# Low part of each head's q on GpSimd, and silu's product ahead of the block's maxima on VectorE, in a kernel of windowed attention and a gated feed-forward

## The chip, the core and the metric

The kernel runs on one core of a Trainium2 chip. The metric is the device time of one execution in microseconds (us), as the median of several runs. Of the core's engines, TensorE (PE) multiplies matrices, VectorE (DVE), ScalarE (ACT) and GpSimd (POOL) do the elementwise work, and SyncE (SP) issues the transfers. Each engine takes its instructions in the order in which the program wrote them for it, and waits at one whose inputs aren't there or whose output space isn't free.

## The reference

Attention over 8 batches, 8 heads, 576 positions and 64 dimensions a head, with a window of 32 positions in the first four heads and of every fourth position in 128 in the others; then a normalised, gated feed-forward over the 4608 tokens of width 512, with 1536 hidden columns:

```python
scores = where(mask, (q @ k.T) / sqrt(64), -1e9)
attn = softmax(scores) @ v                     # -> x: 4608 x 512
rms = sqrt(mean(x * x, -1) + 1e-6)
xn = x / rms * rms_g
g = xn @ w_gate
val = xn @ w_val
out = (g * sigmoid(g) * val) @ w_out
```

All inputs and outputs are float32.

## The kernel before, in words

The 4608 tokens are cut into 16 units of 288 (half a sequence). The feed-forward of unit u runs on TensorE while the attention of unit u + 1 is worked off in between, so the feed-forward of each of the units 2 to 14 has nearly the same pattern in time (even and odd units differ in the number of keys).

**The steps.** The feed-forward of a unit has 12 hidden blocks j of 128 columns, and each block three steps: part 0 is `gate` (the product for g), part 1 is `val`, part 2 is `proj` (the output product of the block before, into four accumulators `acc`). A step of a unit from 1 on is 12 matmuls of 128 x 288: four pieces of 128 rows, times three products. The three come from the way in which float32 is kept: each operand is split into a high part, rounded to the faster type fp32r, and a low part, the rest; high x high, low x high and high x low are added up.

**Attention in between.** After a step's 12 matmuls come those of the attention that are due: scores `s` (L508, L511), transposes `t` of the normalised probabilities (L486), outputs `o` (L495, L499, L500), at the sum of squares `rps` and its spreading `bps` (L601). A unit has 14 attention blocks, begun about every second step. The work of a block: maxima on VectorE (`scores_max`: L379 adds the mask, L384 takes the maximum of each of two heads), exponentials on ScalarE (L395), row sums and reciprocals on VectorE (L404, L405), division on GpSimd (L411), transposition on TensorE, high and low parts of the transposed on ScalarE (L466) and VectorE (L468), and the output: copied by ScalarE (L431), and its second half added by VectorE (L441, in `add`). From unit 3 on (`NEX = 3`) q and k are split too: `split` takes the high parts on ScalarE (L348 for k, L357 for q) and the low parts elsewhere (`k_lo` L353, `q_lo` L362). The q and k of a head come in one transfer with their two copies on 128 partitions; q's low part is wanted on the upper 64 alone, so `q_lo` works on 64 x 288. When `q_lo` is written the transfer of the head two further on is issued too.

**What sets the order.** Nothing is reordered by a scheduler. `later(dt, rank, fn)` puts `fn` on a list for the step dt ahead; at the start of each step `flush` runs that step's list in the order of rank (lower first, equal ranks in the order of entry), before the step's matmuls are written. The ranks that matter here: reciprocals -1, `add` of outputs -0.3, tanh and `prod` 0, transposes' copy 0.2, low part of the transposed 0.4, `normal` and `part` (the normalised input) 0.6, `scores_max` 0.7, `silu` 0.8, `q_lo` 0.9, `k_lo` 5. `tanh`, `silu` and the maxima of a block that was scored in part 0 stand in one flush, that of part 1. For odd j a block is scored in part 0; for even j it is scored elsewhere.

**Who holds what.** `gate` and `val` share two banks of PSUM in turn, and the transposes use the bank that is next free: the bank of gate j is free when `silu` (L697) has read it, then may hold a transposed block until L468 has read that, and is then that of val j + 1. The output `o` has one bank, free when `add` (L441) has read it. `th` holds tanh, then silu, then the product with val (`prod`, L710), and has one buffer: the next tanh waits until the high part (`hhi`, L721 on ScalarE) and the low part (`hlo`, L722 on GpSimd) are taken from it. The input's low parts `xlo` are made in `part` (L633), those of two pieces on VectorE and of two on GpSimd.

The functions that the change touches, and what calls them:

Of the kernel before, what the change touches and what calls it, by code (L numbers as in the profile page):

```python
# [29 lines left out]
NEX = 3  # L30
# [31 lines left out]
def geometry(u, c):  # L62


    half = u % 2
    if c < NC // 2:
        if half:
            return [(QB * i, QB * i, 0, P) for i in range(U // QB)], QB, U + W
        return [(QB * i, max(QB * i - W, 0), 0 if i else W, P if i else QB)
                for i in range(U // QB)], QB, U  # L70
    nq = U // DIL
    keys = nq + (W if half else 0)
    return [(nq * r, keys * r, 0 if half else W, keys) for r in range(DIL)], nq, keys * DIL
# [3 lines left out]
def attn_moe(ctx: ExitStack, tc: tile.TileContext, qk_in, v_in, w_gate, w_val, w_out, rms_g, outT):  # L77
# [4 lines left out]
    V, A, G, PE = nc.vector, nc.scalar, nc.gpsimd, nc.tensor  # L82
# [36 lines left out]
    def later(dt, rank, fn):  # L119
        put_off.setdefault(now[0] + dt, []).append((rank, fn))  # L120
# [164 lines left out]
    def load(u, h):  # L285

        _, _, nkt = geometry(u, h // 2)
        if u < NEX and h % 4 > 1:
            raw = sb.tile([P, 2 * KW], F32, tag="ks", name=f"qk_{u}_{h}", bufs=3)
        else:  # L290
            raw = sb.tile([P, U + KW], F32, tag="qk", name=f"qk_{u}_{h}", bufs=2)
        nc.sync.dma_start(out=raw[:, :U + nkt], in_=qk_in[u, h][:, :U + nkt])
        heads[u, h] = raw
# [35 lines left out]
    def after(u, h, n):  # L329

        k = u * H + h + n
        return divmod(k, H) if k < NU * H else None

    def split(u, h, when, ek, eq):


        raw = heads[u, h]
        _, _, nkt = geometry(u, h // 2)
        qr, kr = raw[:, :U], raw[:, U:U + nkt]
        got = []  # L340

        def tile(cols, tag):
            pool, bufs = (late[0], 1) if late and h % 4 == 3 else (sb, 3)
            return pool.tile([P, cols], F32R, tag=tag, name=f"{tag}_{u}_{h}", bufs=bufs)

        def k_hi():
            ks = tile(2 * KW, "ks").rearrange("p (t k) -> p t k", t=2)
            A.copy(out=ks[:, 0, :nkt], in_=kr)  # L348
            got.append(ks)

        def k_lo():
            ks = got[0]
            ek.tensor_tensor(out=ks[:, 1, :nkt], in0=kr, in1=ks[:, 0, :nkt], op=ALU.subtract)  # L353

        def q_hi():
            qs = tile(U, "qs")
            A.copy(out=qs, in_=qr)  # L357
            got.append(qs)

        def q_lo():  # L360
            ks, qs = got
            eq.tensor_tensor(out=qs[D:], in0=qr[D:], in1=qs[D:], op=ALU.subtract)  # L362
            heads[u, h] = (qs, ks)
            if after(u, h, 2):
                load(*after(u, h, 2))

        for dt, rank, fn in zip(when, (3, 5, 3.1, 0.9 if when[3] > when[2] else 3.2), (k_hi, k_lo, q_hi, q_lo)):
            later(dt, rank, fn)
# [66 lines left out]
    def add(u, c, i, o):  # L435
        _, nq, _ = geometry(u, c)
        x = xraw[u, c]
        to = x[:, QB * i:QB * i + nq] if c < NC // 2 else x.rearrange("p (j r) -> p r j", r=DIL)[:, i, :]
        for a in range(2):
            rows = slice(a * D, (a + 1) * D)  # L440
            V.tensor_tensor(out=to[rows], in0=o[rows, a * nq:(a + 1) * nq], in1=to[rows], op=ALU.add)  # L441
# [31 lines left out]
    def products(q, t, o, t_ps, s_tag="s", o_tag="o", wait=False):  # L473


        if q:
            s_ps = ps.tile([P, 512], F32, tag=s_tag, name=f"s_{q[0]}_{q[1]}_{q[2]}")
        if o:
            o_ps = ps.tile([P, 512], F32, tag=o_tag, name=f"o_{o[0]}_{o[1]}_{o[2]}")
            pt = st.pop(o)  # L480
        if t:
            p, _ = st.pop(t)
        def transposed(a):
            blocks, nq, _ = geometry(*t[:2])
            n = blocks[t[2]][3]
            PE.transpose(t_ps[:n, a * QB:a * QB + nq], p[:nq, a, :n], ident[:nq, :nq])  # L486

        def output(a):
            blocks, nq, _ = geometry(*o[:2])
            n = blocks[o[2]][3]  # L490
            if a:
                return
            out = o_ps[:, :2 * nq].rearrange("d (a q) -> d a q", a=2)
            if o[0] < NEX:
                PE.matmul(out, vs.pop(o)[:n].rearrange("k a d -> k (a d)"), pt[:n, 0, :, :nq], start=True, stop=True)  # L495
                return
            vh, vl = (part[:n].rearrange("k a d -> k (a d)") for part in vparts[everything.index(o) % 2])
            both = o_ps[:, :4 * nq].rearrange("d (t a q) -> d t a q", t=2, a=2)
            PE.matmul(both, vh, pt[:n, :, :, :nq], start=True, stop=False)  # L499
            PE.matmul(out, vl, pt[:n, 0, :, :nq], start=False, stop=True)  # L500

        def scored(a):
            blocks, nq, _ = geometry(*q[:2])
            qc, kc, _, n = blocks[q[2]]
            sv = s_ps[:QB].rearrange("q (a t k) -> q a t k", a=2, t=2)
            if q[0] < NEX:
                qk = heads[q[0], 2 * q[1] + a]
                PE.matmul(sv[:nq, a, 0, :n], qk[:, qc:qc + nq], qk[:, U + kc:U + kc + n], start=True, stop=True)  # L508
                return
            qs, ks = heads[q[0], 2 * q[1] + a]  # L510
            PE.matmul(sv[:nq, a, :, :n], qs[:, qc:qc + nq], ks[:, :, kc:kc + n], start=True, stop=True)  # L511

        order = ((t, transposed), (o, output), (q, scored))
        if t and t[0] >= NEX:
            order = ((o, output), (t, transposed), (q, scored))
        parts = [(b, fn, a) for b, fn in order for a in range(2)]
        for b, fn, a in parts:
            if b:
                fn(a)
        if t:  # L520
            later(1, 0.2, lambda: untranspose(t, t_ps, wait))
        if o:
            later(1, 0.5, lambda: take(*o, o_ps))
            if o[0] >= NEX:
                later(2, -0.3, lambda: add(*o, o_ps))
            if o[0] < NEX:
                later(1, 9, lambda: load_v(further(o, 3)))
            far = further(o, 2)
            if far and far[0] >= NEX:
                split_v(far, 8 if o[0] < NEX else 1)  # L530
        if q:
            later(1, 0.7, lambda: scores_max(*q, s_ps))
            later(2, 2, lambda: scores_exp(*q))
            later(3 if q[0] < NNAT else 4, -1, lambda: scores_norm(*q))
            u, c, i = q
            nxt = after(u, 2 * c, 2)
            nb = len(geometry(u, c)[0])
            if u < NEX:
                if u == NNAT - 1 and c == NC - 1 and i == nb - 1:
                    for h in range(4):  # L540
                        later(1, 9, lambda h=h: load(NNAT, h))
                if u >= NNAT and i == nb - 1 and c < NC - 1:
                    for a in range(2):
                        later(1, 9, lambda a=a: load(*after(u, 2 * c + a, 4)))
                if u == NEX - 1 and c == NC - 1 and i == nb - 1:
                    for a in range(2):
                        later(3 + a, 9, lambda a=a: split(NEX, a, (1, 2, 2, 3), G, V))
            elif nxt and i == 0:
                split(*nxt, (1, 2, 2, 3), G, V)
                split(nxt[0], nxt[1] + 1, (2, 3, 3, 4), G, V)  # L550

    xs = {}
    NB = U // QB
# [125 lines left out]
    def gate(u, j):  # L679
        g_ps = group("g", u, j)  # L680
        if u == 0:
            used.append(("g", j))
        g = g_ps[:, :U]

        def tanh():
            nonlocal g
            t = (sb.tile([P, U], F32, tag="hhi", name=f"h_{j}", bufs=2) if u == 0 else
                 sb.tile([P, U], F32, tag="th", name=f"th_{u}_{j}", bufs=1))
            if u + j == 0:
                g = sb.tile([P, U], F32, tag="hhi", name="g_first", bufs=2)  # L690
                V.tensor_tensor(out=g, in0=g_ps[:, :U], in1=root[0], op=ALU.mult)
            A.activation(out=t, in_=g, func=AF.Tanh, scale=0.5)  # L692
            gv[u, j] = t

        def silu():
            t = gv[u, j]
            V.scalar_tensor_tensor(out=t, in0=t, scalar=1.0, in1=g, op0=ALU.add, op1=ALU.mult)  # L697

        later(1, 0 if u + j else 0.65, tanh)
        later(1, 0.8, silu)  # L700
        return g_ps[:, U:U + 2 * QB]

    def val(u, j):
# [220 lines left out]
```

## Time and profile before

| what | value |
|---|---|
| median of 3 runs | 1148.53 us (1148.25 to 1151.82) |
| profiled execution | 1148.96 us |
| its span, from the first instruction to the last | 1146.8 us, 2.2 us less than its time |
| TensorE busy | 1122.0 us, 98% of the span |
| VectorE, ScalarE, GpSimd busy | 736.7, 702.7 and 597.5 us (64, 61 and 52%) |
| granted TensorE clock | 1.000 throughout |
| DMA engines | 23.5% |

A matmul's time in the profile runs from its start to an end that is modelled, and the next one starts before that end. A stretch in which TensorE was kept waiting thus shows as a start that comes late after the start before it, and the idle time given in brackets is only the part of it that lies behind the modelled end. Times in the rows of a timeline are in us from the start of the span.

### The profile page before, as it was taken

How to read it: one execution, taken by the hardware profiler on the slowest of the kernel's cores; microseconds unless marked ns; L12 is line 12 of the kernel's file. 1: busy time of each engine (PE TensorE's matmuls, PEld its weight loads, DVE VectorE, ACT ScalarE, POOL GpSimd, SP SyncE). 2: the span in 40 equal slices, each digit the busy share in tenths (PEclk: the TensorE clock that was granted, in tenths of full speed). 3: DMA queues.
4: the chain of work that ended last, by engine and by line, in shares of the span. 5: the costliest groups of instructions: out<-in, count | busy, mean ns of one | idle time of the engine just before them, and what ended most of it. 6: DMA issues, size and time to landing. Idle time of an engine off the chain costs nothing.

```text
span 1146.8 us, 25563 instructions
## 1 busy us (share of the span) xinstructions
PE 1122.0 (98%) x8362; PEld 1078.3 (94%) x8362; DVE 736.7 (64%) x2838; ACT 702.7 (61%) x2579; POOL 597.5 (52%) x1050
## 2 busy tenths in 40 slices
PE   7999999999999999999999999999999999999998
PEld 5787999999999999999999999999999999999998
DVE  7889778656575665757656575665757656575412
ACT  6795667657576665756656565665656656565311
POOL 7423577555465554646556465564546555464211
PEclk9999999999999999999999999999999999999999
DMA  9664312212131121212212131131212212120000
GB/s 258 180 250 164 96 45 76 64 33 79 41 99 40 50 84 40 79 41 62 69 39 82 40 92 42 48 90 38 76 40 62 78 34 77 42 79 15 3 19 22
DMA packets 61542, 82.17 MB, mean 72 GB/s; under 512 B 7298, under 2 KB 41090, under 8 KB 61410
## 3 DMA queue, kind: packets, MB, share of 16 engines
q1 hardware_dynamic: 61410, 80.54, 23.5%
q8 instruction: 67, 1.10, 0.4%
q14 instruction: 65, 0.53, 0.2%
HBM read 71.08 MB, written 9.44 MB: 70 GB/s over the span
## 4 chain that ended last, share of the span: by engine, by line
PE 74%; DVE 12%; ACT 7%; POOL 3%; issue 2%; DMA 1%; SPq 0%; DVEq 0%; POOLq 0%; ACTq 0%
PE acc L655 13%; PE g L655 13%; PE v L655 12%; PE acc L652 7%; PE g L652 7%; PE v L652 6%; PE s L511 2%; PE o L499 2%; DVE qs L362 2%; PE acc L649 2%; PE v L649 2%; PE t L486 2%; PE g L649 2%; DVE t L379 2%; DVE t L384 2%
## 5 line engine op out<-in xcount | busy, mean ns | idle before, releaser
L722 POOL TENSOR_TENSOR hlo<-th,hhi 128x288 fp32r<-128x288 f32 x179 | 145.7, 814 | 213.0 <-ACT hhi L721 206.6
L655 PE MATMUL acc<-hhi,lo 128*128 128x288 f32 x720 | 212.6, 295 | 0.0
L411 POOL TENSOR_SCALAR t<-t,sum 72x72 f32<-72x72 f32 (+3 forms) x414 | 151.8, 378 | 67.1 <-DVE sum L405 52.5
L721 ACT CAST hhi<-th 128x288 fp32r<-128x288 f32 x180 | 78.0, 433 | 171.2 <-DVE th L710 171.2
L323 POOL TENSOR_TENSOR vlo<-vt,vhi 128x128 fp32r<-128x128 f32 x182 | 87.2, 479 | 178.8 <-ACT vhi L319 177.3
L655 PE MATMUL g<-xhi,lo 128*128 128x288 f32 x612 | 180.3, 295 | 0.0
L655 PE MATMUL v<-xhi,lo 128*128 128x288 f32 x612 | 180.2, 294 | 0.0
L395 ACT ACTIVATE t<-t,sum 96x128 f32<-96x128 f32 (+3 forms) x448 | 165.2, 372 | 11.4 <-DVE sum L384 10.9
L692 ACT ACTIVATE th<-g 128x288 f32<-128x288 f32 x180 | 73.6, 409 | 127.2 <-PE g L486 72.3
L697 DVE SCALAR_TENSOR_TENSOR th<-th,g 128x288 f32<-128x288 f32 x180 | 81.1, 450 | 92.1 <-ACT th L692 57.9
L655 PEld LDWEIGHTS acc<-hhi,lo 128*128 128x128 f32 x720 | 135.4, 188 | 0.0
L441 DVE TENSOR_TENSOR xraw<-o,xraw 64x72 f32<-64x72 f32 (+1 forms) x364 | 97.1, 267 | 39.0 <-ACT xraw L431 35.9
L655 PEld LDWEIGHTS g<-xhi,lo 128*128 128x128 f32 x612 | 115.2, 188 | 0.0
L655 PEld LDWEIGHTS v<-xhi,lo 128*128 128x128 f32 x612 | 115.1, 188 | 0.0
L379 DVE TENSOR_TENSOR t<-s,mask 96x256 f32<-96x256 f32 (+3 forms) x182 | 66.7, 366 | 73.9 <-PE s L511 63.7
L652 PE MATMUL acc<-hhi,hi_o 128*128 128x288 f32 x360 | 109.1, 303 | 0.0
L652 PE MATMUL g<-xhi,hi_g 128*128 128x288 f32 x357 | 106.9, 300 | 0.8 <-DVE th L710 0.8
L710 DVE TENSOR_TENSOR th<-th,v 128x288 f32<-128x288 f32 x180 | 80.9, 450 | 40.5 <-PE v L655 35.5
L655 PE MATMUL acc<-hlo,hi_o 128*128 128x288 f32 x360 | 106.4, 296 | 0.0
L431 ACT COPY xraw<-o 64x72 f32<-64x72 f32 (+1 forms) x364 | 95.4, 262 | 11.8 <-PE o L500 9.7
L353 POOL TENSOR_TENSOR ks<-qk,ks 128x288 fp32r<-128x288 f32 (+2 forms) x104 | 96.9, 936 | 1.9 <-ACT ks L348 1.6
L655 PE MATMUL g<-xlo,hi_g 128*128 128x288 f32 x322 | 95.1, 295 | 0.0
(188 smaller groups left out, 3525.6 us busy)
## 6 DMA issues: line engine op xcount, KB each, us to landing
qk<-in_qk_dram SPq DMA_DIRECT2D x60, 288.0 KB, 2.9
vt<-in_v_dram SPq DMA_DIRECT2D x196, 64.0 KB, 1.8
qk<-in_qk_dram SPq DMA_DIRECT2D x30, 352.0 KB, 3.0
out_dram<-ot SPq DMA_DIRECT2D x64, 144.0 KB, 1.9
qk<-in_qk_dram SPq DMA_DIRECT2D x30, 304.0 KB, 2.9
raw<-in_w_gate_dram SPq DMA_DIRECT2D x12, 512.0 KB, 6.4
raw<-in_w_val_dram SPq DMA_DIRECT2D x12, 512.0 KB, 6.4
raw<-in_w_out_dram SPq DMA_DIRECT2D x12, 512.0 KB, 4.6
```

Of the source, the lines that this page charges most:

```text
L323: G.tensor_tensor(out=vl, in0=vs.pop(b), in1=vh, op=ALU.subtract)
L353: ek.tensor_tensor(out=ks[:, 1, :nkt], in0=kr, in1=ks[:, 0, :nkt], op=ALU.subtract)
L379: V.tensor_tensor(out=t[:nq, :, :n], in0=sv[:nq, :, 1, :n], in1=mask[:nq, None, mc:mc + n].to_broadcast([nq, 2, n]), op=ALU.add)
L395: A.activation(out=t[:nq, a, :n], in_=t[:nq, a, :n], func=AF.Exp, scale=-1.0, bias=sm[:nq, a, 0:1], accum_out=sm[:nq, a, 1:2] if u or i % ...
L411: (V if u == 0 and (c, i) > (NC - 1, 0) else G).tensor_scalar(out=t[:nq, a, :n], in0=t[:nq, a, :n], scalar1=sm[:nq, a, 3:4], scalar2=1.0, ...
L431: A.copy(out=to[a * D:(a + 1) * D], in_=o[a * D:(a + 1) * D, (2 + a) * nq:(3 + a) * nq])
L441: V.tensor_tensor(out=to[rows], in0=o[rows, a * nq:(a + 1) * nq], in1=to[rows], op=ALU.add)
L652: PE.matmul(out, wh[:, cc, :], xh, start=start, stop=False)
L655: PE.matmul(out, w[:, cc, :], v, start=False, stop=stop and k == 1)
L697: V.scalar_tensor_tensor(out=t, in0=t, scalar=1.0, in1=g, op0=ALU.add, op1=ALU.mult)
L710: V.tensor_tensor(out=t, in0=t, in1=v_ps[:, :U], op=ALU.mult)
L722: (V if (u, j) == (NU - 1, NJ - 1) else G).tensor_tensor(out=lo, in0=t, in1=hi, op=ALU.subtract)
```

## The change

There are two edits. In `split`, the engine that takes q's low part is given by the caller, and in all four calls it becomes GpSimd (`G`) where it was VectorE (`V`). The calls concern units 3 to 15, so 104 instructions. And `silu` gets rank 0.6 where it had 0.8, for all units of the feed-forward but the first, so that it is written ahead of `scores_max` (0.7) where both stand in one flush.

```diff
                     for a in range(2):
-                        later(3 + a, 9, lambda a=a: split(NEX, a, (1, 2, 2, 3), G, V))
+                        later(3 + a, 9, lambda a=a: split(NEX, a, (1, 2, 2, 3), G, G))
             elif nxt and i == 0:
-                split(*nxt, (1, 2, 2, 3), G, V)
-                split(nxt[0], nxt[1] + 1, (2, 3, 3, 4), G, V)
+                split(*nxt, (1, 2, 2, 3), G, G)
+                split(nxt[0], nxt[1] + 1, (2, 3, 3, 4), G, G)
...
         later(1, 0 if u + j else 0.65, tanh)
-        later(1, 0.8, silu)
+        later(1, 0.6 if u else 0.8, silu)
```

What this does to the order in which the instructions stand is seen at three places. The first is VectorE around the last hidden block (j = 11) of a unit, before: the names are those of the program with their buffers' numbers (`th_11` is tanh of block 11, `t_1_1` the scores of piece 1, block 1, `qs_4` the parts of q of head 4, `pt` the transposed, `spare` and `xlo` parts of the next unit's input). Each L384 row stands a second time, for the second head.

```order
L615 SCALAR_TENSOR_TENSOR xraw_3_8603<-xraw_3_8603,gs,bps_8879 128x288
L379 TENSOR_TENSOR t_1_1_8983<-s_1_1_8970,mask 96x256
L384 ISA t_1_1_8983,sum_86<-s_1_1_8970,t_1_1_8983 96x128
L384 ISA sum_86 96x1
L697 SCALAR_TENSOR_TENSOR th_11_8975<-th_11_8975,g_11_8957 128x288
L362 TENSOR_TENSOR qs_4_8954<-qk_4_8798,qs_4_8954 64x288
L404 TENSOR_REDUCE sum_90<-sum_90 96x2
L405 RECIPROCAL sum_90<-sum_90 96x2
L710 TENSOR_TENSOR th_11_8975<-th_11_8975,v_11_8994 128x288
L468 TENSOR_TENSOR pt_0_1_8977<-g_11_8957,pt_0_1_8977 128x192
L633 TENSOR_TENSOR xlo_3_9017<-xraw_3_8603,spare 128x288
L362 TENSOR_TENSOR qs_5_8991<-qk_5_8837,qs_5_8991 64x288
```

And VectorE at the same place with the change:

```order
L615 SCALAR_TENSOR_TENSOR xraw_3_8603<-xraw_3_8603,gs,bps_8879 128x288
L697 SCALAR_TENSOR_TENSOR th_11_8975<-th_11_8975,g_11_8957 128x288
L379 TENSOR_TENSOR t_1_1_8984<-s_1_1_8970,mask 96x256
L384 ISA t_1_1_8984,sum_86<-s_1_1_8970,t_1_1_8984 96x128
L384 ISA sum_86 96x1
L404 TENSOR_REDUCE sum_90<-sum_90 96x2
L405 RECIPROCAL sum_90<-sum_90 96x2
L710 TENSOR_TENSOR th_11_8975<-th_11_8975,v_11_8994 128x288
L468 TENSOR_TENSOR pt_0_1_8977<-g_11_8957,pt_0_1_8977 128x192
L633 TENSOR_TENSOR xlo_3_9017<-xraw_3_8603,spare 128x288
L468 TENSOR_TENSOR pt_0_2_9046<-t_11_9037,pt_0_2_9046 128x192
```

Both L362 are gone, and silu (L697) stands ahead of the maxima, behind the input's normalisation (L615). The same holds for j = 1, 3, 5 and 9; for j = 10 silu passes one L615, and elsewhere silu keeps its place.

The second place is VectorE in block j = 4, where the next chunk's scores begin, before:

```order
L468 TENSOR_TENSOR pt_2_2_9453<-t_3_9444,pt_2_2_9453 104x2x72
L379 TENSOR_TENSOR t_3_1_9460<-s_3_1_9445,mask 72x2x104
L384 ISA t_3_1_9460,sum_88<-s_3_1_9445,t_3_1_9460 72x104
L384 ISA sum_88 72x1
L362 TENSOR_TENSOR qs_0_9429<-qk_0_9196,qs_0_9429 64x288
L404 TENSOR_REDUCE sum_87<-sum_87 72x2
L405 RECIPROCAL sum_87<-sum_87 72x2
L441 TENSOR_TENSOR xraw_2_9457<-o_2_0_9446,xraw_2_9457 64x72 x2
L697 SCALAR_TENSOR_TENSOR th_4_9493<-th_4_9493,g_4_9474 128x288
L362 TENSOR_TENSOR qs_1_9467<-qk_1_9231,qs_1_9467 64x288
L710 TENSOR_TENSOR th_4_9493<-th_4_9493,v_4_9501 128x288
```

With the change the two L362 rows are gone here and nothing else moves: the maxima and silu stand in different flushes. The third place is GpSimd around j = 11, in the changed kernel:

```order
L353 TENSOR_TENSOR ks_4_8927<-qk_4_8798,ks_4_8927 128x416
L633 TENSOR_TENSOR xlo_2_8980<-xraw_2_8358,xhi_2_8979 128x288
L362 TENSOR_TENSOR qs_4_8954<-qk_4_8798,qs_4_8954 64x288
L353 TENSOR_TENSOR ks_5_8952<-qk_5_8837,ks_5_8952 128x416
L411 TENSOR_SCALAR t_1_0_8923<-t_1_0_8923,sum_90 96x128 x2
L722 TENSOR_TENSOR hlo_11_9014<-th_11_8975,hhi_11_9013 128x288
L362 TENSOR_TENSOR qs_5_8991<-qk_5_8837,qs_5_8991 64x288
L323 TENSOR_TENSOR vlo_2278<-vt_0_2_8652,vhi_2277 128x128
```

The two L362 rows are new there: one stands between the low parts of two heads' k, the other behind the low part of the hidden block (L722). The orders of TensorE, ScalarE and SyncE are as before.

## The prediction

> **What bounds the kernel now.** I read the page's first part, then the waits of TensorE, then the timelines of four engines over one pattern of two units, which repeats.
>
> ```profile
> span 1146.8 us, 25563 instructions
> PE 1122.0 (98%) x8362; PEld 1078.3 (94%) x8362; DVE 736.7 (64%) x2838; ACT 702.7 (61%) x2579; POOL 597.5 (52%) x1050
> ...
> PE o L499 <- DVE xraw L441: 4.5, 12, 0.4
> PE bps L601 <- ACT rd L585: 3.1, 13, 0.3
> PE v L652 <- DVE pt L468: 2.4, 7, 0.3
> ```
>
> TensorE is busy 98% of the span, and the change leaves its instructions alone, so all that can be won is time in which it is kept waiting. The waits (total in us, times, longest) come 7, 12 and 13 times, 13 units split q, even and odd in turn: bps waits in all of them, v in the 7 even ones, o in 6 of either kind. They show only what lies behind the modelled end of the matmul before, so I take the lateness from the starts. One pattern, near 600 us, in an even unit ("A"):
>
> ```profile
> 603.53 0.25 PE L500 MATMUL o<-pt,vlo 128*128 128x192 f32 x1
> 603.82 0.36 PE L486 MATMUL t<-ident,t 96*128 96x96 f32 x2
> ...
> 605.71 0.29 PE L655 MATMUL g<-spare,lo 128*128 128x288 f32 x1
> 606.35 0.40 PE L652 MATMUL v<-xhi,hi_g 128*128 128x288 f32 x1 [0.34 <-DVE pt L468]
> ...
> 612.20 0.25 PE L500 MATMUL o<-pt,vlo 128*128 128x192 f32 x1
> 612.29 0.33 PE L486 MATMUL g<-ident,t 96*128 96x96 f32 x2
> ...
> 616.03 0.25 PE L500 MATMUL o<-pt,vlo 128*128 128x192 f32 x1
> 616.34 0.36 PE L486 MATMUL t<-ident,t 96*128 96x96 f32 x2
> ...
> 629.41 0.29 PE L655 MATMUL g<-xlo,hi_g 128*128 128x288 f32 x1
> 629.55 0.29 PE L655 MATMUL g<-spare,lo 128*128 128x288 f32 x1
> 629.92 0.40 PE L652 MATMUL v<-xhi,hi_v 128*128 128x288 f32 x1
> ...
> 631.48 0.29 PE L655 MATMUL v<-spare,lo 128*128 128x288 f32 x1
> 632.14 0.37 PE L499 MATMUL o<-pt,vhi 104*128 104x288 f32 x1 [0.36 <-DVE xraw L441]
> ```
>
> A start follows the last after 0.13-0.14 (629.41 to 629.55), a transpose after 0.09 (612.20 to 612.29). So TensorE comes late by 0.29 - 0.09 = 0.20 at 603.82, 0.64 - 0.13 = 0.51 at 606.35, 0.31 - 0.09 = 0.22 at 616.34, 0.37 - 0.13 = 0.24 at 629.92 and 0.66 - 0.13 = 0.53 at 632.14. In the odd unit ("B") two of the same places:
>
> ```profile
> 675.11 0.29 PE L655 MATMUL g<-xhi,lo 128*128 128x288 f32 x1
> 675.47 0.40 PE L652 MATMUL v<-xhi,hi_g 128*128 128x288 f32 x1
> ...
> 700.03 0.29 PE L655 MATMUL v<-xhi,lo 128*128 128x288 f32 x1
> 700.71 0.37 PE L499 MATMUL o<-pt,vhi 72*128 72x288 f32 x1 [0.39 <-DVE xraw L441]
> ```
>
> 0.36 - 0.13 = 0.23 and 0.68 - 0.13 = 0.55. All these wait for VectorE, whose queue there is:
>
> ```profile
> 600.46 0.42 DVE L379 TENSOR_TENSOR t<-s,mask 96x256 f32<-96x256 f32 x1 [0.58 <-PE s L511]
> ...
> 601.81 0.86 DVE L362 TENSOR_TENSOR qs<-qk,qs 64x288 fp32r<-64x288 f32 x1
> 603.33 0.35 DVE L468 TENSOR_TENSOR pt<-g,pt 128x192 fp32r<-128x192 f32 x1
> 604.24 1.18 DVE L633 TENSOR_TENSOR xlo<-xraw,spare 128x288 fp32r<-128x288 f32 x1 [0.56 <-ACT spare L632]
> 605.45 0.46 DVE L362 TENSOR_TENSOR qs<-qk,qs 64x288 fp32r<-64x288 f32 x1
> 605.94 0.36 DVE L468 TENSOR_TENSOR pt<-t,pt 128x192 fp32r<-128x192 f32 x1
> ...
> 612.92 0.37 DVE L379 TENSOR_TENSOR t<-s,mask 72x208 f32<-72x208 f32 x1 [1.23 <-POOL ks L353]
> ...
> 624.62 0.37 DVE L379 TENSOR_TENSOR t<-s,mask 72x208 f32<-72x208 f32 x1 [1.96 <-PE s L511]
> ...
> 630.67 0.46 DVE L362 TENSOR_TENSOR qs<-qk,qs 64x288 fp32r<-64x288 f32 x1
> 631.16 0.15 DVE L404 TENSOR_REDUCE sum<-sum 72x2 f32<-72x4 f32 x1
> ```
>
> The reader is to see L362 ahead of what TensorE waits for: ahead of both L468 that free the banks (603.33, 605.94), and at 630.67 ahead of the additions that free the output's bank.
>
> **The change part by part: q's low part.** It takes 104 instructions from VectorE, 0.46 each and 0.49 with the handover (630.67 to 631.16), more where it is held up (0.86), and puts 104 on GpSimd:
>
> ```profile
> L362 DVE TENSOR_TENSOR qs<-qk,qs x104: 454/455/1655, 164.3 to 1030.2; 64x288 fp32r<-64x288 f32 x104
> ...
> 600.21 0.41 ACT L692 ACTIVATE th<-g 128x288 f32<-128x288 f32 x1 [0.18 <-PE g L486]
> 612.73 0.41 ACT L692 ACTIVATE th<-g 128x288 f32<-128x288 f32 x1
> 624.41 0.41 ACT L692 ACTIVATE th<-g 128x288 f32<-128x288 f32 x1 [1.79 <-PE g L486]
> ...
> 602.32 1.30 POOL L353 TENSOR_TENSOR ks<-qk,ks 128x416 fp32r<-128x416 f32 x1
> 603.61 0.71 POOL L411 TENSOR_SCALAR t<-t,sum 96x128 f32<-96x128 f32 x2
> 604.29 0.81 POOL L722 TENSOR_TENSOR hlo<-th,hhi 128x288 fp32r<-128x288 f32 x1
> 605.97 0.45 POOL L323 TENSOR_TENSOR vlo<-vt,vhi 128x128 fp32r<-128x128 f32 x1 [0.87 <-ACT vhi L319]
> ```
>
> No subtraction on 64 partitions stands on GpSimd; the nearest row is L722, as many columns, two inputs: 0.81. I take 0.81 (half the partitions could make it 0.4, a hold-up like that of L353 1.3). 104 x 0.81 = 84 us, which makes GpSimd 597.5 + 84 = 682 us, 59%. It lies beside TensorE's work: at the dense place GpSimd gets 1.6 us more between 602 and 606, of which 0.87 was idle; what follows slips by about 0.8. Behind it in GpSimd's queue stand k's low part, the divisions L411 and L722. The first two are read by TensorE two steps or more later (by the steps of the code; a step is 12 starts of 0.13, so over 3 us); L722 must be out before the next tanh, since `th` has one buffer. With a slip of 0.8 it ends near 605.9, and the next block's tanh starts there about 606, so this cover is thin; were it gone, each 0.1 us would be paid by tanh first, and by TensorE only if silu also became late. The transfer that waits for q's buffer leaves as much later, and has four steps before its use.
>
> **Silu ahead.** It removes nothing. Where silu now stands first VectorE waits until tanh ends, plus 0.04. At j = 11 that is 600.21 + 0.41 + 0.04 = 600.66 against 600.46 for the maxima, 0.20 lost; at j = 1 613.18 against 612.92, 0.26; at j = 3 624.86 against 624.62, 0.24. What it could give, a bank free a microsecond sooner, nobody waits for at those blocks. I cost it at these losses.
>
> **The sum, place by place.**
> - j = 11, A. Up to the first L468 VectorE wins 0.86 + 0.03 - 0.20 = 0.7, more than the 0.20 that the transposes are late. Then product, ScalarE's copies and L633 come 0.7 sooner, and the second L362 (0.49) is gone: the second L468 can end over 1 us sooner, against 0.51. Both waits end: 0.71, 7 times: 5.0.
> - j = 1, A: 0.49 - 0.26 = 0.23 against 0.22: gone, 7 x 0.22 = 1.5.
> - j = 3 and 4. At j = 3 there is no L362, and the 0.24 goes through product, ScalarE and L468 to the v at 629.92: that wait grows by 0.24. At j = 4 L362 goes: 0.49 back. Net 0.25 in A, 6 times: 1.5. In B the maxima have fewer keys and start sooner, so I take a loss of 0.30 there and 0.19 net (0.25 at most), 6 times: 1.1.
> - j = 11, B: 0.23, 6 times: 1.4.
> - j = 9: reciprocals, L411 and the root stand behind an L362; 0.49 less a silu wait of 0.20 to 0.26 as above. That would cover the 0.24 of each bps (3.1 / 13), but GpSimd has one q more there; I count 2.0 of 3.1 (bounds 0 and 3.1).
>
> Sum 5.0 + 1.5 + 1.5 + 1.1 + 1.4 + 2.0 = 12.5 us. The profiled execution took 1148.96 us (2.2 outside its span), 0.43 above the median: 1148.96 - 12.5 = 1136.5, and 1136 against the median of 1148.5. If everything named waits no more, A gives 0.20 + 0.51 + 0.22 + 0.24 + 0.53 = 1.7 and B 0.8, with bps 6.5 x 1.7 + 6 x 0.8 + 3.1 = 19: 1129.5. That is the lower bound of the terms.
>
> **Weighed against the Trainium skill.** The row at 604.24 shows VectorE's L633 taking 1.18, where an L362, with two inputs from the same memory and as many columns, takes 0.46; it began before L411 ended (603.61 + 0.71 = 604.32) and ended 0.32 after L722 (605.10). By the Trainium skill's "SBUF — State Buffer", section "Who interferes with whom", a VectorE instruction with two SBUF inputs and a GpSimd one that reads SBUF exclude each other, and whoever issues first has the ports for the whole instruction. The trace agrees on the exclusion, but not on the order: L633 stood first and lost. By that rule L633 gets in at the end of the instruction then running, and the sum stands.
>
> **The rivals.**
> - *The wait only changes its name.* VectorE waits for tanh instead of working, and that costs as much as L362 did. For it: it idles 1.96 and 1.23 there now, so its queue is often short, and what it does is set by others. Against it: the rows at 601.81 and 605.45. If each L362 of 0.46 is made good by a wait of that size there remain the hold-up of 0.4 and part of the j = 4 place, about 13 x 0.35 = 4.5: 1144.
> - *GpSimd's run of work shuts L633 out: slower.* At j = 11 GpSimd would be busy without a break from 602.3 to 606.5 (rows from 602.32, plus two q of 0.81). L633, now ready at 603.5, loses at every boundary as it did at 604.29, and runs at 606.5 to 606.95 (0.46 as L362); L468 follows with 0.36, and v starts at 607.4, not 606.35: 1.05 later, 7 times, and by as much in B, 6 times: 13.7. Against it the other places win 6.1 (12.5 - 5.0 - 1.4): 7.6 slower, 1156. It decides from the third boundary lost on; one has been lost in the rows, and L362 at 601.81 with 0.86 got in after one.
> - *The change is not felt*: GpSimd is late enough that tanh and with it VectorE slip by what they won: 1147 to 1149.
> - *More than the sum*: nearly all named waits go, 1130.
>
> **How the numbers follow.** Forecast 0.58, more 0.12, renamed wait 0.16, not felt 0.06, slower 0.08. A difference of 0.3% (3.4 us) is about what a measurement of this kernel tells from none. The renamed wait straddles that bound, 0.11 to 0.05. Faster 0.58 + 0.12 + 0.11 = 0.81, same 0.05 + 0.06 = 0.11, slower 0.08. The range goes from 1128, under the lower bound of the terms, to 1146, into the renamed wait; the forecast's own is 1131 to 1140.
>
> **What would show it.** Right: v after L468 near 606 and t at 603.8 and 616.3 follow the matmul before at 0.13 and 0.09; o waits under 0.1 at j = 4, v at j = 3 waits 0.4 to 0.5; VectorE idles before L697 for ScalarE's tanh; L362 on GpSimd takes 0.8. Wrong: L633 takes over 1.5 us, tanh waits for L722, or L362 on GpSimd takes 1.2 or more and k's low part reaches the scores late.

## The result, and the profile after

The changed kernel takes 1131.51 us in the median (1130.82 to 1135.33, 4 runs) against 1148.83 (1148.25 to 1151.82, 4 runs) of the kernel before on the same chip: ratio 0.9851, 95% interval 0.9823 to 0.9879. That is 17.3 us or 1.5% faster. The prediction was 1136, its range 1128 to 1146, the forecast's own 1131 to 1140.

The first part of the page of the changed kernel:

```profile
span 1129.7 us, 25452 instructions
PE 1112.0 (98%) x8362; PEld 1078.5 (95%) x8362; DVE 676.2 (60%) x2734; ACT 701.7 (62%) x2579; POOL 674.7 (60%) x1154
```

The span falls by 17.1 us. TensorE's instructions are the same 8362; GpSimd gained 77 us of work and VectorE lost 60. The waits of TensorE in the changed kernel (total us, times, longest):

```profile
PE v L652 <- DVE pt L468: 5.3, 12, 0.5
...
PE t L486 <- DVE pt L468: 0.7, 3, 0.3
...
PE bps L601 <- ACT rd L585: 0.4, 1, 0.4
```

Two of the three kinds of wait are gone: o waited 12 times before and is no longer listed, bps waited 13 times and now once. The third, v for L468, came 7 times with 2.4 us and now comes 12 times with 5.3, in the odd units too. The t is new, and comes in three single units. The changed kernel's timeline of TensorE over the same pattern shows which is which:

```profile
595.03 0.25 PE L500 MATMUL o<-pt,vlo 128*128 128x192 f32 x1
595.12 0.33 PE L486 MATMUL t<-ident,t 96*128 96x96 f32 x2
...
596.99 0.30 PE L655 MATMUL g<-spare,lo 128*128 128x288 f32 x1
597.12 0.29 PE L652 MATMUL v<-xhi,hi_g 128*128 128x288 f32 x1
...
620.08 0.29 PE L655 MATMUL g<-spare,lo 128*128 128x288 f32 x1
620.81 0.40 PE L652 MATMUL v<-xhi,hi_v 128*128 128x288 f32 x1 [0.44 <-DVE pt L468]
621.05 0.29 PE L655 MATMUL v<-spare,hi_v 128*128 128x288 f32 x1
...
622.37 0.29 PE L655 MATMUL v<-spare,lo 128*128 128x288 f32 x1
622.50 0.31 PE L499 MATMUL o<-pt,vhi 104*128 104x288 f32 x1
```

At the dense place t follows at 0.09 and v at 0.13: both waits have ended. At j = 4 o follows at 0.13, where it was late by 0.53. The v ahead of it starts 0.73 after the matmul before, so it is late by 0.60 where it was late by 0.24.

To see every place at once I take the time from the start of one block's first gate product on TensorE to that of the next block. A0 to A11 are the intervals of one even unit, B0 to B11 those of the odd unit that follows. In the kernel before A0 begins at 604.25: v at 606.35 lies in A0, t at 603.82 just ahead of it in B11, the v at 629.92 and the o at 632.14 both in A4, bps in A10 and B10. Intervals in us, of one pattern; those left out differ by at most 0.07:

```
             A0   A1   A3   A4   A5   A10  A11  | B0   B1   B4   B5   B10  B11
before      6.18 6.29 5.90 6.44 5.60 5.87 6.06 | 5.85 6.06 6.31 5.58 5.98 6.08
changed     5.42 6.20 6.01 6.20 5.78 5.42 5.84 | 5.41 6.02 6.06 5.98 5.60 5.85
q alone     5.43 6.05 5.89 5.84 5.62 5.42 5.84 | 5.41 5.97 5.60 5.59 5.46 5.85
silu alone  6.16 6.89 6.02 6.77 5.78 6.28 6.13 | 5.86 6.83 6.79 5.62 6.46 6.14
```

The first two rows are the result: the changed kernel wins in A0, A10, A11, B0, B10 and B11, wins only part of what there is in A1, A4 and B4, and loses in A3 and A5. Its 5.98 in B5 is an exception of the pattern shown: the units 3, 5, 7, 11 and 13 have 5.61 to 5.63 there, against 5.56 to 5.59 before. All other intervals of the table lie within 0.06 of the median of their like in the units 2 to 14. The last two rows belong to the first two experiments, and they say why.

### The profile page after: what moved, and what is told of

It is laid out like the page before. It is cut to its first block, busy times and chain, and to the rows that moved or that the text cites. A ratio compares the mean times of both kernels' runs of the same rounds, so it can differ in the third digit from the quotient of the medians.

```text
span 1129.7 us, 25452 instructions
## 1 busy us (share of the span) xinstructions
PE 1112.0 (98%) x8362; PEld 1078.5 (95%) x8362; DVE 676.2 (60%) x2734; ACT 701.7 (62%) x2579; POOL 674.7 (60%) x1154
## 4 chain that ended last, share of the span: by engine, by line
PE 87%; ACT 5%; DVE 4%; POOL 1%; issue 1%; DMA 1%; SPq 0%; DVEq 0%; ACTq 0%; POOLq 0%
PE g L655 15%; PE acc L655 15%; PE v L655 15%; PE v L652 8%; PE acc L652 8%; PE g L652 8%; PE s L511 3%; PE o L499 2%; PE acc L649 2%; PE v L649 2%; PE t L486 2%; PE g L649 2%; PE o L500 1%; ACT t L395 1%; PE g L486 1%
## 5 line engine op out<-in xcount | busy, mean ns | idle before, releaser
L722 POOL TENSOR_TENSOR hlo<-th,hhi 128x288 fp32r<-128x288 f32 x179 | 145.6, 813 | 177.3 <-ACT hhi L721 160.8
L697 DVE SCALAR_TENSOR_TENSOR th<-th,g 128x288 f32<-128x288 f32 x180 | 81.7, 454 | 210.2 <-ACT pt L466 134.8
L721 ACT CAST hhi<-th 128x288 fp32r<-128x288 f32 x180 | 78.0, 433 | 169.8 <-DVE th L710 169.7
L323 POOL TENSOR_TENSOR vlo<-vt,vhi 128x128 fp32r<-128x128 f32 x182 | 84.5, 464 | 141.9 <-ACT vhi L319 140.8
L692 ACT ACTIVATE th<-g 128x288 f32<-128x288 f32 x180 | 74.1, 412 | 135.8 <-PE g L486 77.3
L710 DVE TENSOR_TENSOR th<-th,v 128x288 f32<-128x288 f32 x180 | 81.0, 450 | 42.2 <-PE v L655 37.5
L431 ACT COPY xraw<-o 64x72 f32<-64x72 f32 (+1 forms) x364 | 95.4, 262 | 11.9 <-PE o L500 9.7
L353 POOL TENSOR_TENSOR ks<-qk,ks 128x288 fp32r<-128x288 f32 (+2 forms) x104 | 94.0, 904 | 4.1
L362 POOL TENSOR_TENSOR qs<-qk,qs 64x288 fp32r<-64x288 f32 x104 | 84.2, 809 | 15.4 <-ACT qs L357 8.7
```

Source lines behind the costliest of these rows:

```text
L323: G.tensor_tensor(out=vl, in0=vs.pop(b), in1=vh, op=ALU.subtract)
L431: A.copy(out=to[a * D:(a + 1) * D], in_=o[a * D:(a + 1) * D, (2 + a) * nq:(3 + a) * nq])
L710: V.tensor_tensor(out=t, in0=t, in1=v_ps[:, :U], op=ALU.mult)
L722: (V if (u, j) == (NU - 1, NJ - 1) else G).tensor_tensor(out=lo, in0=t, in1=hi, op=ALU.subtract)
```

## The experiments

All kernels were timed against the kernel before on their own chip, where it took 1148.19 us (first four) and 1148.61 us (last three). Each diff is against the changed kernel, save where another is named.

**Each part by itself.** First q's low part on GpSimd and silu where it was:

```
-        later(1, 0.6 if u else 0.8, silu)
+        later(1, 0.8, silu)
```

> Only q's low part moves to GpSimd; silu keeps its rank of 0.8, behind the maxima. Theory: the whole gain is q's, and silu ahead is a loss at j = 3, where the changed kernel shows the v matmuls 0.60 us late against 0.24 before. Then v at j = 3 goes back to about 0.25 late in all 13 units and the time is 13 x 0.35 = 4.5 us under the changed kernel's 1131.5: 1127. Rival: silu ahead is what brings the products of j = 11 and j = 1 forward; then those waits (0.2 to 0.5) stay and the time lies between 1136 and 1142.

Measured: 1119.22 us (1118.86 to 1119.86), ratio 0.9746 (0.9733 to 0.9759): 29.0 us faster than before and 12.3 faster than the changed kernel. Then silu ahead and q's low part on VectorE:

```
-                split(*nxt, (1, 2, 2, 3), G, G)
-                split(nxt[0], nxt[1] + 1, (2, 3, 3, 4), G, G)
+                split(*nxt, (1, 2, 2, 3), G, V)
+                split(nxt[0], nxt[1] + 1, (2, 3, 3, 4), G, V)
```

(and the same in the two calls for the first heads of unit 3, the first unit that is split)

> Only silu moves ahead of the maxima; q's low part stays on VectorE. Theory: a loss. Silu starts 0.09 us after ScalarE's copy of the transposed (0.45 to 0.55 after the scores are there), so the chain at j = 3 and 4 comes 0.35 to 0.5 later in 13 units (5 to 6 us), and j = 11 and the root's chain at j = 9 lose 0.3 to 0.5 each (4 to 8 us): 1157 to 1162 against 1148.8 before. Rival: silu ahead alone is worth something, 1140 to 1148.

Measured: 1173.06 us (1172.19 to 1175.67), ratio 1.0218 (1.0204 to 1.0232): 24.9 us slower. Both have the sign that was expected and both are larger. The waits of TensorE with silu alone:

```profile
PE v L652 <- DVE pt L468: 7.6, 19, 0.5
PE o L499 <- DVE xraw L441: 6.9, 25, 0.4
PE bps L601 <- ACT rd L585: 6.8, 13, 0.5
PE t L486 <- DVE pt L468: 3.2, 13, 0.3
```

Every kind of wait of the kernel before is there, longer or more often, and a new one of t. So the change is a gain and a loss together: q's move is worth 29.0 us, and silu's takes 12.3 of them back. It takes only half of its own 24.9, since without L362 VectorE catches up in places where it could not with it: silu costs 0.60 in A1, 0.77 in B1 and 0.41 in A10 by itself (table), and 0.15, 0.05 and nothing where q is on GpSimd.

**Why silu ahead costs more than the wait for tanh.** Silu's row in the list of instruction groups of the changed kernel (the last column is VectorE's idle time ahead of the group and what ended it):

```profile
L697 DVE SCALAR_TENSOR_TENSOR th<-th,g 128x288 f32<-128x288 f32 x180 | 81.7, 454 | 210.2 <-ACT pt L466 134.8 <-ACT th L692 70.9 <-ACT xraw L431 2.1
```

In most of its idle time silu waits not for tanh (L692) but for L466, ScalarE's copy of the transposed probabilities that stands behind tanh. The timelines of TensorE, ScalarE and VectorE of the changed kernel at j = 3, followed to the v that is late:

```profile
614.45 0.29 PE L486 MATMUL g<-ident,t 72*104 72x72 f32 x2
...
614.84 0.41 ACT L692 ACTIVATE th<-g 128x288 f32<-128x288 f32 x1 [1.79 <-PE g L486]
615.14 0.27 ACT L466 CAST pt<-g 104x144 fp32r<-104x144 f32 x1
...
615.50 0.46 DVE L697 SCALAR_TENSOR_TENSOR th<-th,g 128x288 f32<-128x288 f32 x1 [2.42 <-ACT pt L466]
615.88 0.36 DVE L379 TENSOR_TENSOR t<-s,mask 72x208 f32<-72x208 f32 x1
...
617.45 0.46 DVE L710 TENSOR_TENSOR th<-th,v 128x288 f32<-128x288 f32 x1
...
617.94 0.43 ACT L721 CAST hhi<-th 128x288 fp32r<-128x288 f32 x1 [1.50 <-DVE th L710]
...
620.13 0.28 ACT L466 CAST pt<-t 104x144 fp32r<-104x144 f32 x1
...
620.45 0.31 DVE L468 TENSOR_TENSOR pt<-t,pt 104x144 fp32r<-104x144 f32 x1 [2.32 <-ACT pt L466]
```

Tanh ends at 614.84 + 0.41 = 615.25, L466 at 615.14 + 0.27 = 615.41, and silu starts 0.09 after that, at 615.50: 0.66 after tanh's start. Before, the maxima started 0.21 after tanh's start (624.41 to 624.62). So VectorE's work begins 0.45 later here, not 0.24. The first row shows what the two have in common: the transposed block is written into bank g beside the product, before silu has read the product (under "Who holds what" it stood as if the bank were free by then). Tanh, L466 and silu all read bank g, and at j = 9, where no such copy stands behind tanh, silu starts 0.03 after tanh's end. In the timelines of the kernel before the product L710 and the L468 of that place stand at

```profile
626.57 0.45 DVE L710 TENSOR_TENSOR th<-th,v 128x288 f32<-128x288 f32 x1
...
629.56 0.31 DVE L468 TENSOR_TENSOR pt<-t,pt 104x144 fp32r<-104x144 f32 x1 [2.32 <-ACT pt L466]
```

which is 2.16 and 5.15 after tanh's start; in the changed kernel it is 2.61 and 5.61. The 0.45 goes through product, ScalarE's queue from L721 to L466, and L468 undiminished, and v starts 0.36 later against the matmul before it. To test the wait for L466, silu was put ahead of it in the step's order:

```
-        later(1, 0.6 if u else 0.8, silu)
+        later(1, 0.1 if u else 0.8, silu)
```

> The changed kernel with silu's rank 0.1 and not 0.6, so that it is written ahead of ScalarE's copy of the transposed (0.2) too. Theory: in the changed kernel silu starts only after that copy (592.42 against tanh's end at 592.12) because of the place where it is written; written ahead of it, it starts 0.04 after tanh. Then v at j = 3 is 0.30 late, not 0.60, and the time is 13 x 0.3 = 4 us lower, 1127.5. Rival: the wait for that copy is one for the bank itself (copy and silu read the same bank of PSUM); then silu starts as late as before and the time stays at 1131.5.

Measured: 1128.77 us (1128.29 to 1128.94), ratio 0.9828 (0.9814 to 0.9841), 2.7 us faster than the changed kernel. Its timelines at the same place:

```profile
613.39 0.41 ACT L692 ACTIVATE th<-g 128x288 f32<-128x288 f32 x1 [1.80 <-PE g L486]
...
613.84 0.46 DVE L697 SCALAR_TENSOR_TENSOR th<-th,g 128x288 f32<-128x288 f32 x1 [2.20 <-ACT th L692]
...
614.33 0.28 ACT L466 CAST pt<-g 104x144 fp32r<-104x144 f32 x1 [0.52 <-DVE th L697]
```

Silu now starts 0.45 after tanh's start, tanh's 0.41 and 0.04 more, as the prediction had it for the changed kernel, and L466 waits 0.52 for silu. In none of the nine kernels does one of the 79 copies that read bank g overlap a silu: the one that is written first goes first, and the other follows after its end, silu 0.09 later in the rows of the changed kernel, the copy 0.03 later in these. ScalarE's L431, which reads the bank of o, overlaps silu 101 times in the changed kernel. So the wait for L466 comes from the shared bank and the order in which the two are written. The rival was wrong in that silu would start as late as before, but right in that it is a wait for the bank; whether the chip or only the program's semaphores keep the two apart is not shown.

The 2.7 us are not the price of that wait alone; the intervals of the two ratios overlap, and the edit moves silu ahead of one more instruction. At j = 9 that is L453, which completes the next unit's sum of squares, from which the root and bps are made. VectorE and TensorE there, two rows each of the changed kernel, then of this one:

```profile
647.75 0.53 DVE L453 TENSOR_TENSOR sq<-sq,sq 128x288 f32<-128x288 f32 x1 [1.14 <-ACT sq L447]
648.85 0.45 DVE L697 SCALAR_TENSOR_TENSOR th<-th,g 128x288 f32<-128x288 f32 x1 [0.56 <-ACT th L692]
...
653.79 0.43 PE L601 MATMUL bps<-rd,ones 96*128 96x288 f32 x2
654.07 0.30 PE L652 MATMUL v<-xhi,hi_o 128*128 128x288 f32 x1
...
646.98 0.45 DVE L697 SCALAR_TENSOR_TENSOR th<-th,g 128x288 f32<-128x288 f32 x1 [2.22 <-ACT th L692]
647.36 0.45 DVE L453 TENSOR_TENSOR sq<-sq,sq 128x288 f32<-128x288 f32 x1
...
651.96 0.77 PE L601 MATMUL bps<-rd,ones 96*128 96x288 f32 x2
652.57 0.30 PE L652 MATMUL v<-xhi,hi_o 128*128 128x288 f32 x1
```

In the changed kernel L453 runs while VectorE would only wait for tanh; here it stands behind silu, and v comes 0.61 after the first bps instead of 0.28. By its intervals this kernel is as fast as q alone in A1, A3, A5 and B5 (6.05, 5.89, 5.59 and 5.59) and loses 0.24 in A4 and 0.25 in B4, close to what the prediction had for silu behind tanh alone (0.24 and 0.30). The rest of what it loses to q alone lies mainly in A10, B9 and B10 (5.76, 5.90 and 5.85), behind L453.

**Where it is paid.** The same kernel as changed, but at the blocks j = 3 silu stays behind the maxima:

```
-        later(1, 0.6 if u else 0.8, silu)
+        later(1, 0.6 if u and j != 3 else 0.8, silu)
```

> The changed kernel with silu at rank 0.8 at j = 3 alone and 0.6 elsewhere. Theory: j = 3 is the only place where silu ahead costs time, so this is as fast as q alone, 1127. Rival: the loss is spread over j = 1, 3, 5, 9 and 11; then it gains a fifth to a third of that, 1130.

Measured: 1124.09 us (1123.58 to 1125.37), ratio 0.9786 (0.9773 to 0.98). So 7.4 of the 12.3 us are paid behind j = 3, and 4.9 elsewhere: neither the one theory (all of it) nor the rival (an even spread) is right. By its intervals A3, A4 and B4 are then as with q alone (5.89, 5.85 and 5.56), while A1, A5 and B10 stay at 6.20, 5.78 and 5.61, as in the changed kernel.

The exception in B5 is not part of this: in that one unit of the changed kernel silu at 695.37 started 0.60 after tanh's end, where it starts 0.25 after it in unit 11, and the t at 698.06 waited 0.23 for the L468 behind it. What held silu there was not followed.

**The two heads apart.** q alone, but with only the first of the two heads' low parts on GpSimd (diff against q alone):

```
-                split(nxt[0], nxt[1] + 1, (2, 3, 3, 4), G, G)
+                split(nxt[0], nxt[1] + 1, (2, 3, 3, 4), G, V)
```

> Silu as before; of the two heads that are split in a unit's step only the first has its q's low part on GpSimd, the second keeps it on VectorE. In the profile of before the first head's L362 are those at 601.81 and 630.67, the second's those at 605.45 and 632.5. Theory by place: what q's move is worth (29.0 us with both heads) is paid at the places where an L362 stands ahead of what TensorE waits for. The first head's stands ahead of both L468 at j = 11, ahead of the additions at j = 4 and ahead of the copies at j = 1 and of the root at j = 9, so it is worth most: 20 to 24 us, 1124 to 1128. Rival, that any 0.46 us taken from VectorE counts alike: half, 14.5 us, 1133.7.

Measured: 1121.16 us (1120.52 to 1121.8), ratio 0.9757 (0.9742 to 0.9772): 27.5 us faster than before. And only the second head's:

```
-                split(*nxt, (1, 2, 2, 3), G, G)
+                split(*nxt, (1, 2, 2, 3), G, V)
```

> The other half: silu as before, only the second head's q has its low part on GpSimd, the first keeps it on VectorE. Theory by place: the second head's L362 stands ahead of one thing that TensorE waits for, the second L468 at j = 11 (605.45, and 674.6 in the odd unit), so it ends the v waits of 0.51 and 0.23 there, 7 x 0.51 + 6 x 0.23 = 5.0, and part of the bps waits at j = 9: 5 to 10 us, 1138 to 1143. Rival, that any 0.46 us counts alike: 14.5 us, 1133.7. If the two halves add up to more than 29 us, both L362 cover the same waits; if to less, one hides behind the other.

Measured: 1136.74 us (1136.49 to 1138.37), ratio 0.9896 (0.988 to 0.9911): 11.9 us faster. Both halves gave more than the 20 to 24 and the 5 to 10 us expected. That every 0.46 us off VectorE counts alike (1133.7 for each) is refuted by both: it is the place that counts. The halves add up to 39.4, against 29.0 for both, so 10.4 us are covered twice. The intervals show where (us; the rest of the pattern as in the table above, or as before):

```
                A0   A1   A4   A10  A11  | B0   B1   B4   B10  B11
first head     5.48 6.05 5.85 5.42 5.84 | 5.41 5.97 5.55 5.59 5.85
second head    5.56 6.29 6.44 5.62 6.06 | 5.42 6.04 6.30 5.67 6.07
```

In A0 and B0 either half ends nearly the whole of the v wait, and in A10 and B10 either gives half or more. The waits in A1, A4, A11, B4 and B11 end by the first head's L362 alone, the one that stands ahead of both L468 and of the additions.

**How much cover GpSimd has left.** q alone, and ahead of each q's low part one more subtraction on GpSimd that writes the first 288 columns of k's low part again:

```
             ks, qs = got
+            ek.tensor_tensor(out=ks[:, 1, :U], in0=kr[:, :U], in1=ks[:, 0, :U], op=ALU.subtract)
             eq.tensor_tensor(out=qs[D:], in0=qr[D:], in1=qs[D:], op=ALU.subtract)
```

> q's low part of both heads on GpSimd, silu as before (1119.2), and ahead of each of the 104 a second writing of the first 288 columns of k's low part, on GpSimd too: the same values again, about 0.81 us each, 84 us more on GpSimd and nothing else. It measures how much cover GpSimd's queue still has. The prediction called it thin: the tanh after j = 11 waits for L722 already (591.94 after an idle 1.15 in the kernel with q alone), so it starts 0.8 later there. If the cover is as thin as that, TensorE pays 0.2 to 0.4 at each of the 26 such places of the 13 units' j = 11 and j = 4: 5 to 10 us, 1124 to 1130. Rival, that a late tanh is hidden as long as silu stands behind the maxima: under 2 us, 1119 to 1121.

Measured: 1133.7 us (1132.98 to 1134.59), ratio 0.9867 (0.9849 to 0.9885): 14.5 us slower than q alone, more than the thin cover was expected to cost. This kernel's line numbers are one higher from L362 on. Of the groups, the added one and q's low part:

```profile
L362 POOL TENSOR_TENSOR ks<-qk,ks 128x288 fp32r<-128x288 f32 x104 | 84.9, 816 | 2.0
L363 POOL TENSOR_TENSOR qs<-qk,qs 64x288 fp32r<-64x288 f32 x104 | 84.8, 815 | 8.2
```

Of the waits, one of TensorE and one of ScalarE:

```profile
PE s L512 <- POOL qs L363: 3.4, 14, 0.6
...
ACT th L693 <- POOL hlo L723: 43.8, 27, 2.1
```

Tanh waits for L722 (here L723), as was expected (43.8 us; 13.6 with q alone). But TensorE also waits in 14 places for q's low part itself, which was not. By the intervals the loss against q alone lies in A0 (6.18), B0 (5.83), B10 (5.80) and A10 (5.55). In A0 and B0 the scores that read q start 0.38 and 0.36 later after the row before them, at 602.16 and 669.80; the other 0.26 of A0 is a transpose at 601.47, and in B10 a bps is 0.25 later, so q's own scores are about half of the loss. In the kernel with q alone the same q at the dense place, and the scores that read it:

```profile
591.99 0.80 POOL L362 TENSOR_TENSOR qs<-qk,qs 64x288 fp32r<-64x288 f32 x1
...
593.37 0.41 PE L511 MATMUL s<-ks,qs 128*72 128x208 f32 x2
```

It is ready at 592.79, 0.58 before the first of the scores. One more instruction of 0.8 takes that up. So the move of q had 0.6 us to spare there, and in this kernel a second one like it on GpSimd was not free.

## Why the prediction was right, and where it was wrong

The direction was right, and so was the mechanism of q's part: the waits that stood behind an L362 ended at the places named. That the time came within 4.5 us is in part luck, since the sum came out by two sizes that were both too small and work against each other: by the prediction's terms q's move was worth about 16 us (12.5, and 0.24 and 0.30 at j = 3 in 6.5 pairs of units, 3.5, given back to silu), and it was worth 29.0; silu's move was to cost those 3.5, and cost 12.3. 16 - 3.5 = 12.5 was forecast, 29.0 - 12.3 = 16.7 was there (17.3 in the changed kernel's own comparison).

Term by term, in us for a pair of an even and an odd unit, from the table:

- *j = 11, A, 0.71:* right in place and mechanism; 0.76 in A0 and 0.23 in B11, 0.99. Part of the excess is a term that the prediction left out: the matmul after a wait is followed later than others. In the timeline of the kernel before, the row behind the late v at 606.35 is

```profile
606.59 0.29 PE L655 MATMUL v<-spare,hi_g 128*128 128x288 f32 x1
606.72 0.29 PE L655 MATMUL v<-xhi,lo 128*128 128x288 f32 x1
```

  0.24 after it, where all others follow at 0.13. So this wait cost 0.51 + 0.11; the 0.17 that remain of the 0.99 were not followed further.
- *j = 11, B, 0.23:* 0.44 in B0, of which the same 0.11 explains half of the excess. And A11 gives 0.22, which the sum did not have: the odd unit's first transposes stood late too, in the kernel before:

```profile
672.94 0.25 PE L500 MATMUL o<-pt,vlo 96*128 96x192 f32 x1
673.22 0.36 PE L486 MATMUL t<-ident,t 96*128 96x96 f32 x2
```

  0.28 - 0.09 = 0.19. I had listed this wait for the even unit (603.82) and not looked for it in the odd one.
- *j = 9, 2.0 of 3.1, that is 0.15 a unit:* the term that was most mis-sized; 0.45 in A10 and 0.38 in B10, some 5.4 us over 13 units. I took the idle time of the list of waits (3.1 / 13 = 0.24) for the price of a bps, though the prediction says itself that such idle times start only behind the modelled end. By the starts in the timeline before

```profile
593.80 0.29 PE L601 MATMUL bps<-rd,ones 96*128 96x288 f32 x1
594.36 0.40 PE L601 MATMUL bps<-rd,ones 96*128 96x288 f32 x1 [0.26 <-ACT rd L585]
594.59 0.30 PE L652 MATMUL v<-xhi,hi_o 128*128 128x288 f32 x1
```

  the second bps is 0.56 - 0.13 = 0.43 late, and the matmul behind it 0.10 more.
- *j = 1, A, 0.22:* 0.09. With q alone it is 0.24, so the term is right for q; silu takes 0.15 of it, at a place where I took the loss of 0.26 as covered by the 0.49 of L362.
- *j = 3 and 4, 0.25 in A and 0.19 in B:* A4 and B4 win 0.24 and 0.25, but by two sizes that were both too small. With q alone A4 wins 0.60 and B4 0.71, for the o wait of 0.53 and 0.55 and the late row behind it. I had counted the 0.49 of one L362, less silu's loss, as what TensorE gets back, but o and v are two waits: q ended the one, silu lengthened the other, and the gain from the first is no credit against the second. The v wait grew by 0.36 in A (0.24 forecast) and, by the starts in the same two views, by 0.50 in B, from 0.10 to 0.60 (0.30 forecast). And the sum had no loss for A3 and A5, where t follows 0.11 and 0.17 later: A3 to A5 together lose 0.05, so the sign is wrong in A. B3 to B5 win 0.19 with the B5 of the other odd units, and lose 0.17 in the pattern shown. What failed is "silu starts at tanh's end plus 0.04": it started 0.09 after the end of L466, which is written ahead of it and reads the same bank.
- *L362 on GpSimd, 0.81:* measured in the changed kernel

```profile
L362 POOL TENSOR_TENSOR qs<-qk,qs 64x288 fp32r<-64x288 f32 x104 | 84.2, 809 | 15.4 <-ACT qs L357 8.7
```

  0.81 and 84 us, as forecast. It lies beside TensorE's work, as forecast; the cover behind it was thin as I wrote, but I named tanh as the first to pay, and the last experiment shows that q's own scores, with 0.58 to spare, pay as much as all others together.
- *What would show it:* of the signs of "right" t at 0.09, v at 0.13, o under 0.1 and L362 at 0.81 came. VectorE is idle before L697, but for L466 (134.8 us) more than for tanh (70.9), and v at j = 3 is late by 0.60, over the 0.4 to 0.5 named. A sign of "wrong" came too: tanh waits for L722, 9 times and 6.5 us in all, where it never did before, 0.77 of it at the dense place (597.63). With q alone it waits 13.6 us, and TensorE's list has no wait of v, o or t left in the pattern, so this sign alone told nothing of the time.

Of the rivals, the run of GpSimd work that shuts L633 out did not come. In the changed kernel's timelines of GpSimd and VectorE at the dense place

```profile
594.83 1.09 POOL L353 TENSOR_TENSOR ks<-qk,ks 128x416 fp32r<-128x416 f32 x1
595.90 0.93 POOL L411 TENSOR_SCALAR t<-t,sum 96x128 f32<-96x128 f32 x2
...
595.20 1.03 DVE L633 TENSOR_TENSOR xlo<-xraw,spare 128x288 fp32r<-128x288 f32 x1 [0.57 <-ACT spare L632]
```

L633 is held behind one GpSimd instruction, L353 up to 595.92, and ends at 596.23, in time for v at 597.12. That VectorE waits for the GpSimd instruction that stood first is what the Trainium skill's "SBUF — State Buffer", section "Who interferes with whom", says; here the trace agrees, and what decides is that it waited for one and not for three. That the wait only changes its name was true of silu: v at j = 3 is the wait that took the place of o at j = 4. "More than the sum" was nearly right in time for the changed kernel (1130), but for another reason than the one given.

## What to carry to other kernels

Measure a change of two parts as two changes before you read its sum: here a gain of 2.5% hid a loss of 1%, and the version with q's move alone (1119.2 us) beats both kernels. An instruction on an in-order queue is put ahead of others only where its own input is there first; see also which other engine reads the same bank, since what is written ahead of it there goes first, and what else in the queue it passes, since a later step may hang on that. The price of a wait is read from starts, with the row behind it, and two waits in one interval are two terms: what ends one is no credit for the other.

## What was not expected of the hardware

- A subtraction on 64 partitions took as long on GpSimd as one on 128 with the same 288 columns: 809 ns (L362, changed kernel) and 816 ns (the added one of the last experiment). On VectorE the 64 partitions took 455 ns in the kernel before.
- The first 128x288 matmul after a wait shows 0.40 us, not 0.29, and the next starts 0.23 to 0.24 after it, not 0.13. Each such wait costs TensorE some 0.1 us more than its own lateness.
- Silu on VectorE and the copy L466 on ScalarE, which only read different columns of the same bank, never overlapped in any of the nine kernels (79 copies in each), while silu and L431, which reads another bank, did 101 times in the changed kernel. Written behind L466 silu started 0.09 us after its end; written ahead of it silu started 0.04 after tanh, and L466 0.03 after silu's end.
